# Moving PSUM copies to an idle engine, splitting the first loads and using a second PSUM bank in a four-layer attention kernel

## The chip, the cores and the metric

The kernel runs on one NeuronCore of one Trainium2 chip. The metric is the device time of one execution in microseconds (us); lower is better. Before the change it was 2143.56 us, the median of 12 runs (2141.75 to 2147.53). The profile has a row for each engine; they run side by side and meet at semaphores: PE (matmuls), with its weight loads in a row of their own (PEld), DVE (VectorE), ACT (ScalarE), POOL (GpSimd); SP issues the transfers. The program gives each engine one list. In the traces below VectorE and ScalarE work theirs off in order, so an instruction that waits also holds up what stands behind it.

## The reference

```python
S, D, H = 2048, 512, 32                       # head size 16
x = x + A(layernorm(x))                        # softmax attention, one K and V for all 32 heads
x = x + B(layernorm(x))                        # linear attention
x = x + A(layernorm(x)); x = x + B(layernorm(x))
# A: o = softmax(q k^T / 4) v, then @ wo
# B: phi(t) = where(t > 0, t + 1, exp(t)) + 1e-6
#    kv = phi(k)^T v ; z = sum phi(k) ; o = phi(q) kv / (phi(q) z + 1e-6), then @ wo
```

A block A needs 32 x 2048 x 2048 exponentials; in both kernels ScalarE does all of them. A block B has no such loop.

## The kernel before

The program first builds a plan: every operation is added with an engine, a planned time `tau` and the events that it waits for; then each engine's list is sorted by `tau` and emitted. The planned times only set the order; the semaphores decide the real times. The time line of one execution is: first prologue (layernorm, transposes, projections of all 16 tiles of 128 rows), attention loop, tail (preparation of B for the last tile), B main merged with the second prologue, second loop, second tail, final B main.

The loads: x is one transfer, and every projection waits for `ev_w`, the last of all weights.

```python
    ev_x = add(SP, 0.0, lambda e: e.dma_start(x_sb[:], xv), s_xdma, 16)
    ev_x.tau = 8.0
    add(SP, 0.01, ... wk_sb ...); add(SP, 0.02, ... wv_sb ...); add(SP, 0.03, ... wq_sb ...)
    # ... cut: wo_sb, wqkv_sb ...
    ev_w = add(SP, 0.06, lambda e: e.dma_start(wo2_sb[:], ...), s_wdma, 16)
    ev_w.tau = 12.0
```

PSUM is the memory that the matmuls write; the kernel uses it as banks 0 to 7. A session is a group of matmuls into one PSUM bank, and the instructions that read the bank ("readers"). A chain object orders the sessions of one bank: the next one waits for the last reader. In the prologue all copies out of PSUM are VectorE's.

```python
    def proj_session(chain, tau, mml, ncols, w_mm, readers):
        tp = chain.start_tau(_tmax(tau, list(w_mm)))
        # ... cut: 4 matmuls that accumulate into bank(chain.bank) ...
        for (eng, dtau, fn, sem_, xw) in readers:
            tr = _tmax(tr + dtau, [evm] + list(xw))
            evr = add(eng, tr, ..., sem_, waits=[evm] + list(xw))
            evs.append(evr)
        chain.last = evs[-1]
```

The nonlinearity `phi` of B: VectorE reads the bank twice (min, max), ScalarE takes the exponential of the min, VectorE adds. All sessions of the preparation of B use bank 7, because during the loop banks 0 to 5 hold scores and bank 6 the accumulator.

```python
        evs = proj_session(chain, _tmax(tau, w_m), mml, 512, w_mm, [
            (DV, 0.0, ... m_buf = min(src, 0) ...), (DV, D_EVQ, ... r_buf = max(src, 0) + 1e-6 ...)])
        ev_e = add(AC, ..., e.activation(e_buf[:, s, :], m_buf[:, s, :], ACTF.Exp), ac_a, waits=w_e)
        ev_add = add(DV, ..., dst = e_buf + r_buf, dv_a, waits=[ev_e, ev_r])
```

B main: 64 matmuls sum kv over all tiles, VectorE masks the result, and then for each tile: numerator and denominator (PE), two reciprocals and two products (DVE), four transposes (PE), a copy (DVE), the output projection (PE), the addition to x (DVE).

```python
        for g in range(NG8):
            for t in range(T):       # 64 matmuls, they wait for all of pk, v and pq
                ev_kvz = add(PE, tk, ... matmul(kvz_ap(g), lhsT=pk_tok[...], rhs=vaugB[...]) ...)
        # ... cut: mask, then for each tile t: ...
            evc = add(DV, ..., e.tensor_copy(OT_sb[:, t % 2, :, :], tpv), dv_a, waits=wc)
            # ... cut: 4 projection matmuls into bank 5 ...
            evx = add(DV, ..., x_sb[:, t, :] += bank(5), dv_x, waits=[evy])
```

The softmax here doesn't subtract the row's maximum and nothing guards it: scores larger than these inputs give would overflow.

Of the kernel before, what the change touches and what calls it, by code (L numbers as in the profile page):

```python
# [1 line left out]

# [37 lines left out]
class _Sched:  # L40
# [37 lines left out]
    def plan(self, tau, fn):  # L78
        heapq.heappush(self.heap, (float(tau), self.hseq, fn))
        self.hseq += 1  # L80

    def run(self):
        while self.heap:
            tau, _, fn = heapq.heappop(self.heap)
            fn()
# [39 lines left out]
def bass_interleave_layers__grouped_kv_mqa__linear_attn_block__prompt_kernel(  # L125
# [12 lines left out]
    P = 128  # L138
# [8 lines left out]
    EPS = 1e-3  # L147
    HOP = 0.25
# [89 lines left out]
    ev_x = add(SP, 0.0, lambda e: e.dma_start(x_sb[:], xv), s_xdma, 16)  # L238
    ev_x.tau = 8.0
    add(SP, 0.01, lambda e: e.dma_start(wk_sb[:], A_wk.rearrange("(ft f) c -> f ft c", f=P)), s_wdma, 16)  # L240
    add(SP, 0.02, lambda e: e.dma_start(wv_sb[:], A_wv.rearrange("(ft f) c -> f ft c", f=P)), s_wdma, 16)
    add(SP, 0.03, lambda e: e.dma_start(wq_sb[:], A_wq.rearrange("(ft f) c -> f ft c", f=P)), s_wdma, 16)
    add(SP, 0.04, lambda e: e.dma_start(wo_sb[:], A_wo.rearrange("(g r) c -> r g c", r=P)), s_wdma, 16)
    add(SP, 0.05, lambda e: e.dma_start(wqkv_sb[:], B_wqkv.rearrange("(ft f) c -> f ft c", f=P)), s_wdma, 16)
    ev_w = add(SP, 0.06, lambda e: e.dma_start(wo2_sb[:], B_wo.rearrange("(g r) c -> r g c", r=P)), s_wdma, 16)
    ev_w.tau = 12.0
# [20 lines left out]
    t_ = 12.5  # L267
    ev_wkrep = None
    for ft in range(FT):
        ev_wkrep = add(PO, t_, lambda e, ft=ft: e.tensor_copy(  # L270
            wk_rep[:, ft, :].rearrange("p (r d) -> p r d", r=8),
            wk_sb[:, ft, :].unsqueeze(1).to_broadcast([P, 8, DH])), po_a, waits=[ev_w] if ft == 0 else [])
        t_ += 0.5
# [3 lines left out]
    def ln_tile(t, x_ev, tau, chain):  # L277
        tau = _tmax(tau, [x_ev])
        ev1 = add(DV, tau, lambda e, t=t: e.bn_stats(stats[:, t, 0:6], x_sb[:, t, :]), dv_a, waits=[x_ev])  # L279
        ev2 = add(DV, tau + 0.7, lambda e, t=t: e.bn_aggr(mv[:, t, :], stats[:, t, 0:6]), dv_a, waits=[ev1])  # L280
        ev3 = add(DV, tau + 0.95, lambda e, t=t: e.tensor_scalar(out=veps[:, t:t + 1], in0=mv[:, t, 1:2], scalar1=1e-5, scalar2=None,  # L281
                                                             op0=ALU.add), dv_a, waits=[ev2])
        ev4 = add(PO, _tmax(tau + 1.35, [ev3, ev_mhalf]), lambda e, t=t: e.tensor_tensor(out=rstd[:, t:t + 1], in0=veps[:, t:t + 1], in1=mhalf[:, 0:1], op=ALU.pow),  # L283
                  po_a, waits=[ev3, ev_mhalf])
        slot = t % 2
        wr = ln_state["xn_last_reader"][slot]
        tx = _tmax(tau + 2.2, [ev4, wr])
        ev5 = add(DV, tx, lambda e, t=t, slot=slot: e.tensor_scalar(  # L288
            out=xn_buf[:, slot, :], in0=x_sb[:, t, :], scalar1=mv[:, t, 0:1], scalar2=rstd[:, t:t + 1],
            op0=ALU.subtract, op1=ALU.mult), dv_a, waits=[ev4, wr])  # L290
        tp = chain.start_tau(_tmax(tx + 0.4 + HOP, [ev5, ev_ident]))
        tpv = bank_bf(chain.bank)
        evt = None
        w0 = [ev5, chain.last, ev_ident]
        for ft in range(FT):
            evt = add(PE, tp + ft * EPS, (lambda e, ft=ft, slot=slot, tpv=tpv: e.transpose(tpv[:, ft, :], xn_buf[:, slot, ft * P:(ft + 1) * P], ident[:])),  # L296
                      pe_a if ft == FT - 1 else None, waits=(w0 if ft == 0 else []))
        ln_state["xn_last_reader"][slot] = evt
        evc = add(DV, evt.tau + 0.7 + HOP, lambda e, t=t, tpv=tpv: e.tensor_copy(xnT[:, :, t * P:(t + 1) * P], tpv), dv_a, waits=[evt])  # L299
        chain.last = evc  # L300
        return evc

    def proj_session(chain, tau, mml, ncols, w_mm, readers):
        tp = chain.start_tau(_tmax(tau, list(w_mm)))
        dst = bank(chain.bank, ncols)
        n = len(mml)
        evm = None
        w0 = [chain.last] + list(w_mm)
        for k, (l, r) in enumerate(mml):
            evm = add(PE, tp + k * EPS, (lambda e, l=l, r=r, k=k, n=n, dst=dst: e.matmul(dst, lhsT=l, rhs=r, start=(k == 0), stop=(k == n - 1))),  # L310
                      pe_a if k == n - 1 else None, waits=(w0 if k == 0 else []))
        evs = []
        tr = tp + n * min(D_MM, 0.05 + ncols * 0.0004) + HOP
        for (eng, dtau, fn, sem_, xw) in readers:
            tr = _tmax(tr + dtau, [evm] + list(xw))
            evr = add(eng, tr, (lambda e, fn=fn, dst=dst: fn(e, dst)), sem_, waits=[evm] + list(xw))
            evs.append(evr)
        chain.last = evs[-1]
        return evs

    def a_prologue(x_evs, tau0, R):
# [4 lines left out]
        chains = [chain6, chain7]  # L326

        def tile_task(t, tau_t):
            ch = chains[t % 2]
            ev_xnT = ln_tile(t, x_evs[t], tau_t, ch)  # L330
            R["xnT"][t] = ev_xnT
            mml = [(xnT[:, ft, t * P:(t + 1) * P], wv_sb[:, ft, :]) for ft in range(FT)]
            evs = proj_session(ch, ev_xnT.tau + HOP, mml, DH, [ev_xnT, ev_w],
                               [(DV, 0.0, (lambda e, src, t=t: e.tensor_copy(Vaug[:, t, 0:DH], src)), dv_a, [ev_ones])])
            R["V"][t] = evs[0]
            if t % 4 == 3:
                b = t // 4
                plan(ev_xnT.tau + HOP, lambda b=b: block_task(b))

        def block_task(b):  # L340
            xw = [R["xnT"][tt] for tt in range(4 * b, 4 * b + 4)] + [ev_w, ev_wkrep]
            tq = _tmax(0, xw, d=HOP)
            for g in range(NG8):
                chq = chains[(g + b) % 2]
                mml = [(wq_sb[:, ft, g * P:(g + 1) * P], xnT[:, ft, b * 512:(b + 1) * 512]) for ft in range(FT)]
                evs = proj_session(chq, tq, mml, 512, xw,
                                   [(DV, 0.0, (lambda e, src, g=g, b=b: e.tensor_copy(QT_sb[:, g, b * 512:(b + 1) * 512], src)), dv_a, [])])  # L347
                R["QT"][(g, b)] = evs[0]
                tq += 0.6
# [3 lines left out]
                               [(DV, 0.0, (lambda e, src, b=b: e.tensor_copy(Krep_sb[:, b * 512:(b + 1) * 512], src)), dv_a, [])])  # L353
            R["Krep"][b] = evs[0]

        for t in range(T):
            tau_t = max(tau0 + 1.7 * t, x_evs[t].tau + HOP)
# [9 lines left out]
    def a_loop(R, L0, on_x, pre_wait):  # L367
# [18 lines left out]
        def tau_seg(j):  # L386
            return L0 + (j + 1) * TG + 0.05

# [138 lines left out]
    def phi_session(chain, tau, mml, dst_ap, w_mm, act_slack):  # L527
# [5 lines left out]
        evs = proj_session(chain, _tmax(tau, w_m), mml, 512, w_mm, [  # L533
            (DV, 0.0, (lambda e, src, s=s: e.tensor_scalar(out=m_buf[:, s, :], in0=src, scalar1=0.0, scalar2=None, op0=ALU.min)), dv_a, w_m),  # L534
            (DV, D_EVQ, (lambda e, src, s=s: e.tensor_scalar(out=r_buf[:, s, :], in0=src, scalar1=0.0, scalar2=1e-6, op0=ALU.max, op1=ALU.add)), dv_a, []),  # L535
        ])
        ev_m, ev_r = evs
        w_e = [ev_m] + ([prev] if prev is not None else [])
        ev_e = add(AC, _tmax(ev_m.tau + act_slack, w_e), (lambda e, s=s: e.activation(e_buf[:, s, :], m_buf[:, s, :], ACTF.Exp)), ac_a, waits=w_e)  # L539
        ev_add = add(DV, _tmax(ev_e.tau + 0.7 + HOP, [ev_e, ev_r]), (lambda e, s=s, dst_ap=dst_ap: e.tensor_tensor(  # L540
            out=dst_ap, in0=e_buf[:, s, :], in1=r_buf[:, s, :], op=ALU.add)), dv_a, waits=[ev_e, ev_r])
        bstate["phi_last"][s] = ev_add
        return ev_add

    def b_prep_tile(t, x_ev, RB, act_slack, gap):
# [4 lines left out]

        def task_k():
            ev_xnT = RB["xnT"][t]
# [4 lines left out]
        def task_v():  # L557
# [3 lines left out]
                (DV, 0.0, (lambda e, src, t=t: e.tensor_copy(vaugB_v[:, t, :, 0:DH], src.rearrange("p (h d) -> p h d", d=DH))), dv_a, [ev_onesB])])  # L561
# [22 lines left out]
    def b_main(RB, tau0, prev_epi, x_out, on_x):  # L584
# [26 lines left out]
        for t in range(T):  # L611
# [4 lines left out]
            tb0 = _tmax(B0 + t * DB, w)  # L616
# [13 lines left out]
            td = _tmax(evnd.tau + 4 * 0.11 + HOP, wd)  # L630
# [12 lines left out]
            if t >= 1:  # L643
                wt.append(cp_ev[t - 1])
            tt = _tmax(evmul.tau + HOP, wt)
            tpv = bank_bf(4)
# [12 lines left out]
            evc = add(DV, _tmax(evt.tau + 0.7 + HOP, wc), (lambda e, t=t, tpv=tpv: e.tensor_copy(OT_sb[:, t % 2, :, :], tpv)), dv_a, waits=wc)  # L659
# [4 lines left out]
            ty = _tmax(evc.tau + HOP, wy)  # L664
# [6 lines left out]
            evx = add(DV, evy.tau + 4 * D_MM + HOP, (lambda e, t=t: e.tensor_tensor(out=x_sb[:, t, :], in0=x_sb[:, t, :], in1=bank(5), op=ALU.add)),  # L671
# [7 lines left out]
    x_evs = [ev_x] * T  # L679
    tau = 9.0  # L680
    prev_epi = {}
    i = 0
    while i < len(layers):
        L = layers[i]
        if L == "A":
# [6 lines left out]
            if nextB:  # L692
                def on_x(qt, evx, RB=RB):
                    b_prep_tile(qt, evx, RB, act_slack=8.0, gap=1.0)
# [7 lines left out]
            if nextB:  # L702
                tau0 = max(max(e.tau for e in x_evs) + 1.0, bprep_end(RB) + 0.5)
                x_out = [None] * T
                b_main(RB, tau0, prev_epi, x_out, None)
# [63 lines left out]
```

## Time and profile before

The stage table gives, for each stretch between two marks of the timeline, its length, and the busy time and the number of instructions of PE, PEld, DVE, ACT and POOL; then the clock that was granted to PE (1.00 is full), the busy share of the DMA engines and GB/s. The marks are: the first exponential of 128x1536, the last normalisation of the loop, the first masking of kv. Where two instructions of an engine overlap, the time counts once. An engine that goes from instruction to instruction can show a little under 100%, for the short gaps before an instruction that needs the result of the last one. The stage table of the kernel before:

```profile
0.00:68.20 68.20, 37.33 (x212) 16.73 (x213) 39.42 (x118) 1.30 (x2) 15.83 (x32) 0.90 0.24 78
68.20:1011.70 943.50, 788.74 (x10585) 468.92 (x10583) 200.22 (x583) 936.19 (x710) 8.24 (x15) 1.00 0.01 2
1011.70:1047.20 35.50, 20.75 (x100) 9.89 (x100) 13.51 (x25) 3.15 (x5) 0.55 (x1) 0.52 0.00 0
1047.20:1124.30 77.10, 56.00 (x405) 26.89 (x405) 69.55 (x218) 0.00 (x0) 8.80 (x16) 0.96 0.00 1
1124.30:2067.90 943.60, 788.77 (x10585) 468.86 (x10583) 200.25 (x584) 936.20 (x710) 8.24 (x15) 1.00 0.01 2
2067.90:2102.30 34.40, 19.68 (x100) 9.34 (x100) 13.48 (x26) 3.15 (x5) 0.55 (x1) 0.55 0.00 0
2102.30:2142.50 40.20, 26.90 (x192) 12.24 (x192) 34.86 (x100) 0.00 (x0) 0.00 (x0) 0.99 0.16 53
```

What to see: in the two loops (943.5 us each) ACT is busy for 936 us. They are bound by the exponentials. The other five stretches sum to 255.4 us, and ACT does nothing in them except the few exponentials of `phi` in the tails: 0.00 us in both B mains. DVE is the busy engine instead: 69.55 of 77.1 us, 34.86 of 40.2 us. The same on the page's rows, where each digit is the busy share of a fortieth of the span in tenths:

```profile
DVE  5221222112322232111680222322213121321227
ACT  0799999999999999998009999999999999999960
```

The first prologue: when PE's first projection starts, and what it waited for. The columns of a timeline line are the start, the duration, engine, line, operation, output<-input, shapes and, in brackets, the idle time of the engine before it and what ended it. Two lines of the timeline of the kernel before:

```profile
9.71 0.69 DVE L279 BATCH_NORM_STATS2 stats<-x_sb 128x6 f32<-128x512 bf16 x1 [9.71 <-DMA x_sb<-in_A_x_dram]
...
18.38 0.25 PE L310 MATMUL ps_all<-wv_sb,xnT 128*128 128x16 bf16 x4 [5.82 <-DMA wo_sb<-in_B_wo_dram]
```

x was there at 9.71, but the V projection of tile 0 waited until 18.38 for a weight that only the output projections of B need.

One session of the first tail, timeline of the kernel before:

```profile
1028.58 1.89 PE L310 MATMUL ps_all<-xnT,wqkv_sb 128*128 128x512 bf16 x4 [1.38 <-DVE r_buf L535]
...
1030.50 0.69 DVE L534 TENSOR_SCALAR m_buf<-ps_all 128x512 f32<-128x512 f32 x1 [1.98 <-PE ps_all L310]
1031.11 0.68 DVE L535 TENSOR_SCALAR r_buf<-ps_all 128x512 f32<-128x512 f32 x1
1031.23 0.63 ACT L539 ACTIVATE e_buf<-m_buf 128x512 f32<-128x512 f32 x1 [2.64 <-DVE m_buf L534]
...
1031.85 1.89 PE L310 MATMUL ps_all<-xnT,wqkv_sb 128*128 128x512 bf16 x4 [1.38 <-DVE r_buf L535]
```

Matmul 1.89 us, min 0.69, max 0.68, next matmul: 3.27 us from one to the next, all in a row, at a granted clock of 0.50. The exponential runs beside it and is hidden.

The merged stage, one long stretch of the stage table of the kernel before: DVE 49.40 of 50 us.

```profile
1060.00:1110.00 50.00, 38.15 (x293) 18.84 (x294) 49.40 (x162) 0.00 (x0) 7.15 (x13) 1.00 0.00 1
```

The final B main, timeline of the kernel before: from one copy to the next 2.18 us, and DVE goes from instruction to instruction.

```profile
2133.80 0.42 DVE L659 COPY OT_sb<-ps_all 128x512 bf16<-128x512 bf16 x1
...
2135.98 0.42 DVE L659 COPY OT_sb<-ps_all 128x512 bf16<-128x512 bf16 x1
```

### The profile page before, as it was taken

How to read it: one execution, taken by the hardware profiler on the slowest of the kernel's cores; microseconds unless marked ns; L12 is line 12 of the kernel's file. 1: busy time of each engine (PE TensorE's matmuls, PEld its weight loads, DVE VectorE, ACT ScalarE, POOL GpSimd, SP SyncE). 2: the span in 40 equal slices, each digit the busy share in tenths (PEclk: the TensorE clock that was granted, in tenths of full speed). 3: DMA queues.
4: the chain of work that ended last, by engine and by line, in shares of the span. 5: the costliest groups of instructions: out<-in, count | busy, mean ns of one | idle time of the engine just before them, and what ended most of it. 6: DMA issues, size and time to landing. Idle time of an engine off the chain costs nothing.

```text
span 2142.5 us, 49091 instructions
## 1 busy us (share of the span) xinstructions
PE 1738.2 (81%) x22176; PEld 1012.9 (47%) x22176; DVE 571.3 (27%) x1648; ACT 1880.0 (88%) x1431; POOL 42.2 (2%) x80
## 2 busy tenths in 40 slices
PE   4888888888888888887678888888888888888876
PEld 2454554445454554544334544544544454444533
DVE  5221222112322232111680222322213121321227
ACT  0799999999999999998009999999999999999960
POOL 2000000000000000000010000000000000000000
PEclk9999999999999999999799999999999999999988
DMA  3000000000000000000000000000000000000001
GB/s 99 1 2 2 2 2 2 2 2 1 2 2 2 2 2 2 2 1 2 1 1 2 2 1 2 2 2 1 2 2 1 2 2 2 1 2 2 1 1 40
DMA packets 7745, 10.50 MB, mean 5 GB/s; under 512 B 1392, under 2 KB 7024, under 8 KB 7536
## 3 DMA queue, kind: packets, MB, share of 16 engines
q1 hardware_dynamic: 7536, 7.37, 1.1%
q8 instruction: 173, 2.83, 0.6%
q14 instruction: 36, 0.29, 0.0%
HBM read 5.28 MB, written 2.10 MB: 3 GB/s over the span
## 4 chain that ended last, share of the span: by engine, by line
ACT 42%; PE 37%; issue 11%; DVE 9%; DMA 0%; SPq 0%; POOL 0%; ACTq 0%; POOLq 0%
ACT PT L433 41%; PE ps_all L423 21%; PE ps_all L452 8%; PE ps_all L310 5%; PE ps_all L508 1%; ACT e_buf L539 1%; DVE Osb L637 1%; DVE Osb L475 1%; DVE x_sb L671 1%; DVE rdenA L469 1%; DVE stats L279 1%; DVE QT_sb L347 1%; PE ps_all L593 1%; DVE rdenB L635 1%; PE ps_all L296 0%
## 5 line engine op out<-in xcount | busy, mean ns | idle before, releaser
L433 ACT ACTIVATE PT<-ps_all 128x1536 bf16<-128x1536 f32 (+1 forms) x1366 | 1851.5, 1490 | 165.8 <-PE ps_all L423 163.9
L423 PE MATMUL ps_all<-qbd,Krep_sb 128*128 128x512 bf16 x4096 | 1114.8, 381 | 215.4 <-ACT PT L433 215.2
L452 PEld LDWEIGHTS ps_all<-Vaug,PT 128*128 128x128 bf16 x16384 | 619.6, 96 | 432.8 <-DVE Osb L475 110.8
L452 PE MATMUL ps_all<-Vaug,PT 128*128 128x17 bf16 x16384 | 639.9, 171 | 93.0 <-DVE Osb L475 91.1
L423 PEld LDWEIGHTS ps_all<-qbd,Krep_sb 128*128 128x128 bf16 x4096 | 301.2, 97 | 488.7 <-ACT PT L433 269.0
L469 DVE RECIPROCAL rdenA<-ps_all 128x4 f32<-128x4 f32 x256 | 46.7, 183 | 1152.1 <-PE ps_all L452 1152.1
L406 DVE TENSOR_TENSOR qbd<-QT_sb,mask 128x512 bf16<-128x512 bf16 x256 | 102.3, 415 | 0.0
L539 ACT ACTIVATE e_buf<-m_buf 128x512 f32<-128x512 f32 x64 | 41.3, 646 | 47.1 <-DVE m_buf L534 47.1
L283 POOL TENSOR_TENSOR rstd<-veps,mhalf 128x1 f32<-128x1 f32 x64 | 35.2, 550 | 2024.4 <-DVE veps L281 2014.8
L310 PE MATMUL ps_all<-wqkv_sb,xnT 128*128 128x512 bf16 x256 | 68.9, 393 | 3.8 <-DVE r_buf L535 2.8
L534 DVE TENSOR_SCALAR m_buf<-ps_all 128x512 f32<-128x512 f32 x64 | 44.2, 690 | 82.3 <-PE ps_all L310 82.3
L475 DVE TENSOR_TENSOR Osb<-ps_all,rdenA 128x64 bf16<-128x64 f32 x256 | 57.4, 224 | 8.9
L540 DVE TENSOR_TENSOR pk_tok<-e_buf,r_buf 128x512 bf16<-128x512 f32 x32 | 22.1, 691 | 104.2 <-ACT e_buf L539 104.2
L310 PE MATMUL ps_all<-xnT,wqkv_sb 128*128 128x512 bf16 x128 | 39.8, 441 | 11.0 <-DVE r_buf L535 9.1
L279 DVE BATCH_NORM_STATS2 stats<-x_sb 128x6 f32<-128x512 bf16 x64 | 44.1, 689 | 10.9 <-DMA x_sb<-in_A_x_dram 9.7
L310 PE MATMUL ps_all<-xnT,wq_sb 128*128 128x512 bf16 x128 | 41.1, 465 | 6.9 <-DVE QT_sb L347 3.4
L296 PE MATMUL ps_all<-ident,xn_buf 128*128 128x128 bf16 x256 | 27.6, 236 | 22.4 <-DVE xn_buf L288 19.4
L535 DVE TENSOR_SCALAR r_buf<-ps_all 128x512 f32<-128x512 f32 x64 | 43.5, 680 | 0.0
L667 PE MATMUL ps_all<-wo_sb,OT_sb 128*128 128x512 bf16 x128 | 33.1, 381 | 9.2 <-DVE OT_sb L659 9.2
L508 PE MATMUL ps_all<-wo_sb,OT_sb 128*128 128x512 bf16 x128 | 33.9, 388 | 1.0 <-DVE OT_sb L496 1.0
L511 DVE TENSOR_TENSOR x_sb<-x_sb,ps_all 128x512 bf16<-128x512 bf16 x32 | 22.0, 687 | 46.7 <-PE ps_all L508 46.7
L299 DVE COPY xnT<-ps_all 128x512 bf16<-128x512 bf16 x64 | 26.1, 408 | 24.7 <-PE ps_all L296 24.7
(46 smaller groups left out, 417.9 us busy)
## 6 DMA issues: line engine op xcount, KB each, us to landing
x_sb<-in_A_x_dram SPq DMA_DIRECT2D x1, 2048.0 KB, 8.9
out_dram<-x_sb SPq DMA_DIRECT2D x16, 128.0 KB, 1.7
wqkv_sb<-in_B_wqkv_dram SPq DMA_DIRECT2D x1, 1536.0 KB, 8.9
wq_sb<-in_A_wq_dram SPq DMA_DIRECT2D x1, 512.0 KB, 6.5
wo_sb<-in_A_wo_dram SPq DMA_DIRECT2D x1, 512.0 KB, 6.5
wo_sb<-in_B_wo_dram SPq DMA_DIRECT2D x1, 512.0 KB, 9.2
wk_sb<-in_A_wk_dram SPq DMA_DIRECT2D x1, 16.0 KB, 8.3
wv_sb<-in_A_wv_dram SPq DMA_DIRECT2D x1, 16.0 KB, 6.7
```

The source lines that it names most:

```text
L279: ev1 = add(DV, tau, lambda e, t=t: e.bn_stats(stats[:, t, 0:6], x_sb[:, t, :]), dv_a, waits=[x_ev])
L310: evm = add(PE, tp + k * EPS, (lambda e, l=l, r=r, k=k, n=n, dst=dst: e.matmul(dst, lhsT=l, rhs=r, start=(k == 0), stop=(k == n - 1))), pe ...
L406: qbd_ready[u] = add(DV, tq, (lambda e, u=u, qt=qt, g=g, half=half: e.tensor_tensor(out=qbd[:, u % NQBD, :].rearrange("p (a b) -> p a b", ...
L423: ev = add(PE, tsi, (lambda e, dst=dst, t=t, u=u: e.matmul(dst, lhsT=Krep_sb[:, t * P:(t + 1) * P], rhs=qbd[:, u % NQBD, :], start=True, s ...
L433: e_done[j] = add(AC, _tmax(tau_E(j), w), (lambda e, j=j, ng=ng, b0=b0: e.activation(PT[:, j % NPT, 0:ng * 512], bank(b0, ng * 512), ACTF. ...
L452: ev = add(PE, tpv, (lambda e, col0=col0, j=j, idx=idx, hh=hh, t=t: e.matmul(ps_all[:, col0:col0 + 17], lhsT=PT[:, j % NPT, idx * 512 + hh ...
L469: evr = add(DV, tn, (lambda e, accv=accv: e.reciprocal(rdenA[:, :].unsqueeze(2), accv[:, :, DH:DH + 1])), dv_a, waits=[ev_acc])
L475: acc_free[u] = add(DV, _tmax(tn + EPS / 4, wn, d=EPS / 8), (lambda e, qt=qt, quad=quad, accv=accv: e.tensor_tensor(out=Osb[:, qt % 2, qua ...
L508: evy = add(PE, t2 + g * EPS, (lambda e, g=g, qt=qt: e.matmul(bank(7), lhsT=OT_sb[:, qt % 2, g, :], rhs=wo_sb[:, g, :], start=(g == 0), st ...
L534: (DV, 0.0, (lambda e, src, s=s: e.tensor_scalar(out=m_buf[:, s, :], in0=src, scalar1=0.0, scalar2=None, op0=ALU.min)), dv_a, w_m),
L535: (DV, D_EVQ, (lambda e, src, s=s: e.tensor_scalar(out=r_buf[:, s, :], in0=src, scalar1=0.0, scalar2=1e-6, op0=ALU.max, op1=ALU.add)), dv_ ...
L539: ev_e = add(AC, _tmax(ev_m.tau + act_slack, w_e), (lambda e, s=s: e.activation(e_buf[:, s, :], m_buf[:, s, :], ACTF.Exp)), ac_a, waits=w_e)
```

## The change

The intent is to use the idle ScalarE and PSUM banks outside the loops, and to start earlier:

1. x comes in four transfers; V, Q and K of A wait only for wk, wv and wq, which are issued before the rest of x; the plan starts earlier.
2. Copies out of PSUM (xnT, V, Q, K, the transposed output of B) go to ScalarE where the plan says that it is free, which is everywhere except from 2 us ahead of a loop to its end.
3. In the tails, `phi` uses relu (the max with 0) on ScalarE, and two banks alternate.
4. The final B main lets the transposes lag two tiles, with two banks for them, and shifts some planned times.

Two smaller edits to the plan are not in the cut below: the tiles of a prologue are planned 1.35 us apart instead of 1.7, and for the last tiles of a loop the planned distances of the preparation of B are shortened (`gap` 1.0 to 0.2, `act_slack` 8.0 to 0.3).

The heap code, rewritten by hand, runs when the program is built; it costs no device time.

```diff
+    act_busy = []
+    def act_free(tau):
+        for (a, b) in act_busy:
+            if a - 2.0 <= tau <= b:
+                return False
+        return True
+    def copy_op(tau, out_ap_fn, waits, prefer_act=True):
+        if prefer_act and act_free(tau):
+            return add(AC, tau, lambda e: out_ap_fn(e, True), ac_a, waits=waits)
+        return add(DV, tau, lambda e: out_ap_fn(e, False), dv_a, waits=waits)
-    ev_x = add(SP, 0.0, lambda e: e.dma_start(x_sb[:], xv), s_xdma, 16)
+    x_chunk(0, 0.0)
     # wk, wv
+    ev_wa = add(SP, 0.03, ... wq_sb ..., s_wdma, 16)
+    for c in range(1, 4):
+        x_chunk(c, 0.03 + 0.001 * c)
     # wo, wqkv, wo2 on another semaphore: ev_w
-        evc = add(DV, evt.tau + 0.7 + HOP, ... tensor_copy(xnT ...) ..., dv_a, waits=[evt])
+        evc = copy_op(evt.tau + 0.7 + HOP, cp, [evt])
     # ... cut: the same for V, Q, K; ev_wa in place of ev_w ...
+        L_end = tau_E(NGR) + 0.5
+        act_busy.append((L0, L_end))
+        if act_free(tau):                                       # phi, in the tails
+            evs = proj_session(chain, tau, mml, 512, w_mm, [
+                (AC, 0.0, ... r_buf = Relu(src) ..., ac_a, w_m),
+                (DV, 0.6, ... m_buf = min(src, 0) ..., dv_a, w_m),
+            ], serial=True)                                     # min waits for relu
+            # exp of m_buf on ScalarE, then DVE: dst = (e_buf + 1e-6) + r_buf
+        def task_tail():                                        # last tile
+            chT = Chain(0)
+            chT.last = astate["e_done"][-1]
+            chs = [chain7, chT]
+            # k on chs[0], v on chs[1], the four q on chs[g % 2]
     # B main
-            tpv = bank_bf(4)
+            tpv = bank_bf(4 if not final or t % 2 == 0 else 6)
-            evc = add(DV, ..., tensor_copy(OT_sb ...), dv_a, waits=wc)
+            evc = copy_op(..., OT_sb ..., wc)
     # ... cut: with final, the wait cp_ev[t - 2] for cp_ev[t - 1], and planned times shifted ...
```

## The prediction

> **What bounds it now.** The timeline splits the 2142.5 us into: first prologue 0 to 68.2 (the first 128x1536 exponential starts there), attention loop 68.2 to 1011.3, tail of linear-attention preparation 1011 to 1048, B main merged with the second prologue 1048 to 1124, loop 1124 to 2067, second tail to 2103, final B main to 2142. In both loops ScalarE is 10.0 of 10 us busy (stretch table), 1.345 us per exponential group. The change leaves the loops alone: inside them its guard sends copies back to VectorE. All gain must come from the other 256 us.
>
> **Step by step.**
>
> 1. First prologue. PE waits 5.8 us for the last weight DMA (wait list): tile 0's V matmul could start at 18.4 although its x was there at 9.7. After: x in four chunks, and V/Q/K wait only for wk, wv, wq. wq landed 11.5 behind 2 MB of x; behind 0.5 MB I estimate 9 to 9.5. Gain about 9. From there the 16 tiles took 50 us, 3.1 each, with VectorE about 75% busy. The 52 PSUM copies (0.41, 0.17, 0.69 us) go to an idle ScalarE. Its exponential of 128x512 takes 0.65 us; the Trainium skill, "ScalarE: Activation LUTs", What ACT_TABLE_LOAD costs, gives 186 ns + 0.833 ns per element, 0.61 us, for any function; so I take 0.6. The two PSUM banks then bind: per four tiles and bank, two tiles at 1.9 us and 2.5 projections at 1.75 (warm PE) to 2.55 (cold): 2.05 to 2.55 per tile; with in-order stalls 2.5. Loop starts near 50: gain 18.
>
> 2. Each tail. Six projection sessions share bank 7: 1.89 us of cold matmul, then two 0.69 us VectorE reads, 3.27 us per session (timeline); 21.5 us from first projection to the kv matmuls. After: two banks alternate, so the matmul hides, but relu (0.63), min (0.69) and exp (0.65) form a serial loop over ScalarE and VectorE of about 2.0 us per session. I estimate 14.5: gain 7 each, plus about 0.5 if a denser PE runs the kv matmuls (6.3 us) at a higher clock. The skill, "TensorE: Matmul & The Clock Gate", Part 1, says sustained activity releases the half clock; the trace agrees: 1.89 us for four 512-column matmuls at granted clock 0.5 in the tail, 1.04 at 1.0 after it.
>
> 3. B main with second prologue. VectorE is 95 to 100% busy from 1050 to 1110, 3.9 us per tile. The change moves about 1.4 us per tile (at the pitch of back-to-back instructions, 0.33, 0.33, 0.09, 0.6) to ScalarE: VectorE's floor falls to 42 us of 62, but PE's own work is about as long, so stalls appear. I expect 50. The last block's 14 us to the loop stays. Gain 12.
>
> 4. Final B main. VectorE bound, 2.17 us per tile; less the 0.33 us copy, 1.84, if the two-tile lag hides latency. Gain 4.
>
> Sum 18+14+1+12+4 = 49: **2095 us**, 8-in-10 range 2076 to 2116. Chances: faster by over 2% 0.70, within 2% 0.29, slower 0.01.
>
> **Right if:** first big exponential near 50; first to last of the tail 7 shorter; loops still 943 each; in B main VectorE at 80 to 90%, no longer 100%; matmuls then wait for ScalarE copies.
>
> **Wrong if:** wq lands later than 10; PE stays cold throughout the prologue (loop start 55); in-order ScalarE or PE queues in the merged stage stall one another (gain under 8) or overlap perfectly (up to 19); relu/copy cause extra table loads (1.28 us each); the tail's new loop is cheaper, PE warming, or dearer because min waits for relu; the final lag brings stalls.

## The result, and the profile after

The changed kernel took 2095.84 us, the median of 8 runs (2095.18 to 2096.96). The ratio of times is 0.9778 (95% interval 0.9768 to 0.9787). The stage table of the changed kernel, with the same marks:

```profile
0.00:49.30 49.30, 33.05 (x213) 15.52 (x214) 20.45 (x67) 23.70 (x54) 15.46 (x32) 0.93 0.34 108
49.30:992.80 943.50, 788.72 (x10585) 468.83 (x10583) 199.48 (x580) 936.16 (x710) 8.24 (x15) 1.00 0.01 2
992.80:1020.10 27.30, 16.54 (x100) 9.29 (x100) 9.63 (x19) 6.86 (x12) 0.55 (x1) 0.69 0.00 1
1020.10:1086.10 66.00, 51.88 (x404) 27.61 (x405) 49.43 (x151) 31.38 (x68) 8.79 (x16) 0.95 0.00 1
1086.10:2029.70 943.60, 788.71 (x10585) 468.82 (x10583) 199.54 (x581) 936.20 (x710) 8.24 (x15) 1.00 0.01 2
2029.70:2057.10 27.40, 17.12 (x100) 9.88 (x100) 9.56 (x18) 6.86 (x12) 0.55 (x1) 0.69 0.00 1
2057.10:2093.70 36.60, 25.13 (x192) 13.49 (x192) 30.36 (x84) 9.38 (x16) 0.00 (x0) 1.00 0.17 58
```

Each line answers to the same line of before:

| stretch | before, us | after, us | difference | predicted |
|---|---|---|---|---|
| first prologue | 68.2 | 49.3 | -18.9 | -18 |
| two loops | 943.5, 943.6 | 943.5, 943.6 | 0 | 0 |
| two tails, with the kv matmuls | 35.5, 34.4 | 27.3, 27.4 | -15.2 | -15 |
| B main merged with second prologue | 77.1 | 66.0 | -11.1 | -12 |
| final B main | 40.2 | 36.6 | -3.6 | -4 |

The page's rows of the changed kernel:

```profile
DVE  3022232111321232111641122322113122322116
ACT  5999999999999999999369999999999999999982
```

The first digit of ACT went from 0 to 5, and the two slices in the middle (the 20th and 21st) from 0 0 to 3 6: ScalarE now works there, and the second loop, too, begins within the later of the two. In the first prologue (timeline of the changed kernel):

```profile
5.00 1.29 DVE L328 BATCH_NORM_STATS2 stats<-x_sb 128x6 f32<-128x512 bf16 x2 [5.00 <-DMA x_sb<-in_A_x_dram]
...
9.09 0.28 PE L363 MATMUL ps_all<-wv_sb,xnT 128*128 128x16 bf16 x4 [0.20 <-ACT xnT L350]
```

Layernorm starts at 5.00 instead of 9.71 and V at 9.09 instead of 18.38. What V waits for now is no longer a transfer but the ScalarE copy of its own input.

A little more than one session of the first tail (timeline of the changed kernel):

```profile
1007.17 0.58 ACT L609 ACTIVATE r_buf<-ps_all 128x512 f32<-128x512 f32 x1
...
1007.90 0.68 DVE L610 TENSOR_SCALAR m_buf<-ps_all 128x512 f32<-128x512 f32 x1
1008.62 0.63 ACT L614 ACTIVATE e_buf<-m_buf 128x512 f32<-128x512 f32 x1 [0.87 <-DVE m_buf L610]
...
1008.64 1.04 PE L363 MATMUL ps_all<-xnT,wqkv_sb 128*128 128x512 bf16 x4 [0.95 <-DVE m_buf L610]
1009.16 0.58 ACT L609 ACTIVATE r_buf<-ps_all 128x512 f32<-128x512 f32 x1
1009.28 0.69 DVE L615 SCALAR_TENSOR_TENSOR pqT<-e_buf,r_buf 128x512 bf16<-128x512 f32 x1 [0.70 <-ACT e_buf L614]
1009.89 0.68 DVE L610 TENSOR_SCALAR m_buf<-ps_all 128x512 f32<-128x512 f32 x1
1010.61 0.63 ACT L614 ACTIVATE e_buf<-m_buf 128x512 f32<-128x512 f32 x1 [0.87 <-DVE m_buf L610]
```

The matmul (1.04 us, at the full clock by now) runs beside the readers. Relu 1007.17, min 1007.90, exp 1008.62, next relu 1009.16: 1.99 us, as forecast. But look at which wait ends last for the next min, at 1009.89. It stands without a gap behind the add of 1009.28, which waited for exp. The relu of its bank had ended at 1009.74; hand-overs between these two engines cost 0.03 to 0.04 us here (min to exp, exp to add), so the relu was out of the way about 0.1 us early. The loop that binds is min, exp, add, and the next min behind the add in VectorE's order: 0.72 + 0.66 + 0.61 = 1.99 us. The relu only nearly binds.

The merged stage, two stretches of the stage table of the changed kernel; the first without a projection block, the second with one:

```profile
1028.40:1040.20 11.80, 7.88 (x83) 4.63 (x81) 11.52 (x37) 5.36 (x12) 2.20 (x4) 1.00 0.01 1
1040.20:1060.00 19.80, 18.69 (x148) 10.20 (x146) 17.63 (x55) 11.51 (x25) 3.30 (x6) 1.00 0.00 1
```

In the first, DVE is busy for 11.52 of 11.8 us and PE for 7.88. In the second PE is busy for 18.69 of 19.8 us and DVE for 17.63. The limit alternates.

The final B main, timeline of the changed kernel:

```profile
2072.50 0.59 ACT L766 COPY OT_sb<-ps_all 128x512 bf16<-128x512 bf16 x1 [1.31 <-PE ps_all L756]
...
2074.39 0.59 ACT L766 COPY OT_sb<-ps_all 128x512 bf16<-128x512 bf16 x1 [1.30 <-PE ps_all L756]
```

From copy to copy 1.89 us, where it was 2.18.

### The profile page after: what moved, and what is told of

It is laid out like the page before. It is cut to its first block, busy times and chain, and to the rows that moved or that the text cites. A ratio compares the mean times of both kernels' runs of the same rounds, so it can differ in the third digit from the quotient of the medians.

```text
span 2093.7 us, 49127 instructions
## 1 busy us (share of the span) xinstructions
PE 1721.1 (82%) x22176; PEld 1013.4 (48%) x22176; DVE 518.4 (25%) x1498; ACT 1950.5 (93%) x1581; POOL 41.8 (2%) x80
## 4 chain that ended last, share of the span: by engine, by line
ACT 44%; PE 39%; issue 11%; DVE 5%; DMA 0%; POOL 0%; ACTq 0%; POOLq 0%; DVEq 0%
ACT PT L506 42%; PE ps_all L496 22%; PE ps_all L525 8%; PE ps_all L363 5%; PE ps_all L581 1%; ACT e_buf L624 1%; DVE Osb L548 1%; DVE Osb L743 1%; DVE rdenA L542 1%; DVE x_sb L778 1%; PE ps_all L345 1%; PE ps_all L699 1%; PE ps_all L774 1%; ACT xnT L350 0%; DVE rdenB L741 0%
## 5 line engine op out<-in xcount | busy, mean ns | idle before, releaser
L542 DVE RECIPROCAL rdenA<-ps_all 128x4 f32<-128x4 f32 x256 | 46.7, 183 | 1174.6 <-PE ps_all L525 1174.6
L363 PE MATMUL ps_all<-wqkv_sb,xnT 128*128 128x512 bf16 x256 | 68.6, 393 | 1.4 <-ACT xnT L350 1.4
L766 ACT COPY OT_sb<-ps_all 128x512 bf16<-128x512 bf16 x32 | 18.9, 589 | 48.6 <-PE ps_all L756 48.5
L619 DVE TENSOR_SCALAR m_buf<-ps_all 128x512 f32<-128x512 f32 x54 | 37.3, 690 | 63.7 <-PE ps_all L363 63.7
L350 ACT COPY xnT<-ps_all 128x512 bf16<-128x512 bf16 x34 | 19.8, 588 | 27.3 <-PE ps_all L345 27.0
L363 PE MATMUL ps_all<-xnT,wqkv_sb 128*128 128x512 bf16 x128 | 34.3, 395 | 3.9 <-DVE m_buf L610 2.8
L620 DVE TENSOR_SCALAR r_buf<-ps_all 128x512 f32<-128x512 f32 x54 | 36.7, 680 | 0.0
L624 ACT ACTIVATE e_buf<-m_buf 128x512 f32<-128x512 f32 x54 | 35.0, 648 | 0.0
```

Of the source, the lines that this page charges most:

```text
L363: evm = add(PE, tp + k * eps, (lambda e, l=l, r=r, k=k, n=n, dst=dst: e.matmul(dst, lhsT=l, rhs=r, start=(k == 0), stop=(k == n - 1))), pe ...
L542: evr = add(DV, tn, (lambda e, accv=accv: e.reciprocal(rdenA[:, :].unsqueeze(2), accv[:, :, DH:DH + 1])), dv_a, waits=[ev_acc])
L624: ev_e = add(AC, _tmax(ev_m.tau + act_slack, w_e), (lambda e, s=s: e.activation(e_buf[:, s, :], m_buf[:, s, :], ACTF.Exp)), ac_a, waits=w_e)
```

## The experiments

Twelve kernels ran, all correct. Ten are the changed kernel with one edit, the eleventh joins three edits, and the last is the changed kernel again. They were run on several chips, each beside the kernel before on the same chip, so the ratios compare best; stage times are from one profiled execution each. Stages that an edit does not touch varied from profile to profile: the first prologue from 48.7 to 50.9 us, the merged stage from 63.7 to 66.7, the final stage from 36.6 to 38.0. For the merged stage this goes in part with the clock granted in its last 13 us, where PE computes the last projections ahead of the loop: 0.74 in the trace of the changed kernel (66.0 us), 0.87 in its second (65.4; other runs at 0.87 up to 66.7), 1.00 in the run with one bank in the tail (63.7). A difference of a stage below 2 us is therefore not taken as shown by one profile.

### First prologue: loads undone

```diff
-    x_chunk(0, 0.0)
+    ev_x = add(SP, 0.0, lambda e: e.dma_start(x_sb[:], xv), s_xdma, 16)
+    ev_x.tau = 8.0
+    x_dma_evs.extend([ev_x] * T)
-    for c in range(1, 4):
-        x_chunk(c, 0.03 + 0.001 * c)
-    ev_w.tau = 16.0
+    ev_w.tau = 12.0
+    ev_wa = ev_w
     # ... cut: all weights on one semaphore, a planned time, the test for the first prologue ...
-    tau = 3.0
+    tau = 9.0
```

> The changed kernel with the old loads: x as one transfer, every projection waiting for the last weight, the old start times in the plan; the copies stay on ScalarE. Theory (start and copies are two separate gains in the first prologue): V can start only at 18.4 instead of 9.1, and the 40.2 us from there to the loop stay, so the first big exponential comes at about 58 instead of 49.3, and the whole takes about 9 us more than the changed kernel (about 2105). Rival (the copies alone did it, the start is hidden): first big exponential within 2 us of 49.3.

Measured: 2104.61 us, ratio 0.9817 (0.9803 to 0.9832). PE's V projection waits for the last weight again, and the first big exponential comes at 60.14 (timeline of this run):

```profile
18.30 0.25 PE L364 MATMUL ps_all<-wv_sb,xnT 128*128 128x16 bf16 x4 [5.82 <-DMA wo_sb<-in_B_wo_dram]
...
60.14 2.79 ACT L507 ACTIVATE PT<-ps_all 128x1536 bf16<-128x1536 f32 x2
```

The loads are worth 10.9 us of the prologue (60.14 - 49.27) and 8.8 us of the whole (2104.61 - 2095.84). The copies did not do it alone.

### First prologue: copies on VectorE

```diff
-    act_busy = []
+    act_busy = [(0.0, 1e9)]
-        act_busy.append((L0, L_end))
+        act_busy[:] = [(L0, L_end)]
```

> The changed kernel with the first prologue's 52 PSUM copies on VectorE again; the new loads stay. Theory (two separate gains): the old pace of 3.1 us per tile from 9.1 on, first big exponential at about 59, whole about 2105. Rival (the two PSUM banks alone set the pace; a VectorE copy is no longer than a ScalarE copy, and VectorE was only 75% busy): first big exponential within 3 us of 49.3.

Measured: 2103.89 us, ratio 0.9812 (0.9797 to 0.9826). The stage table of the run, from V to the first big exponential at 58.45:

```profile
9.00:58.40 49.40, 35.39 (x206) 15.76 (x205) 35.01 (x106) 0.00 (x0) 8.24 (x18) 0.86 0.19 67
```

The first V projection came at 9.49, as early as in the changed kernel, but the pace is the old one: (58.45 - 9.49) / 16 = 3.06 us per tile. So the copies are worth 9.2 us of the prologue (8.1 of the whole), although a copy of xnT takes 0.59 us on ScalarE against 0.41 on VectorE, and although VectorE was busy for a little over two thirds of the stretch. The rival, which looked at the banks and the durations alone, falls. What fits is that a copy on VectorE must also wait its turn among the layernorms of later tiles, while the bank and PE wait for it. The traces show this wait: from the end of the matmuls that a copy reads to its start, the 52 copies waited 19.3 us in sum in this run, 13.7 in the kernel before, 4.7 in the changed kernel (the copies of xnT 0.66 us each in this run, 0.08 in the changed kernel). By duration alone the move would not pay: the 16 copies of xnT are longer on ScalarE by 2.9 us in sum, the 20 of 512 columns in fp32 shorter by 2.0. That this queue, and nothing else, is the cause was not tested by itself. The two parts, 10.9 and 9.2, add up to 20.1, near the 18.9 that the change gained.

### Tail: one bank

```diff
-            chs = [chain7, chT]
+            chs = [chain7, chain7]
```

> The changed kernel with all six sessions of each tail in the one PSUM bank again; relu stays on ScalarE. Theory (the second bank hides the matmul, that is the gain): per session 1.89 cold matmul, relu 0.6, min 0.69 and hops, about 3.3 us; from first projection to the kv matmuls 20 to 21.5 us instead of 13.8, whole about 14 us more (2110). Rival (moving relu off VectorE was the gain): 16 us or less, whole at most 5 us more.

Measured: 2109.37 us, ratio 0.9841 (0.9824 to 0.9857). From the first projection to the kv matmuls 20.94 us in both tails, where the changed kernel has 13.84 and 14.23. With one bank, relu on ScalarE gains 0.6 us per tail over the kernel before (21.51). The second bank is the gain; this run keeps the shortened planned distances, so these are not.

### Tail: two banks, both reads on VectorE

```diff
-        if act_free(tau):
+        if False:
             evs = proj_session(chain, tau, mml, 512, w_mm, [   # relu on ScalarE
```

> The changed kernel with two banks in the tail, but min and max both on VectorE as before, and the addition as before. Theory (the second bank is the gain, and relu on ScalarE only trades one serial loop for another): VectorE has three instructions of about 0.61 pitch per session, 1.83, against the 1.98 measured for relu-min-exp; from first projection to the kv matmuls 12 to 14.5 us, whole within 3 us of the changed kernel. Rival (relu on ScalarE is worth its 0.6 us per session): 3 to 4 us more per tail, whole 6 to 8 us more.

Measured: 2096.3 us, ratio 0.9777 (0.9762 to 0.9791), the same as the changed kernel. First projection to kv matmuls 12.98 and 13.56 us, 0.9 and 0.7 less than the changed kernel's. One session (timeline of this run):

```profile
1006.68 0.68 DVE L619 TENSOR_SCALAR m_buf<-ps_all 128x512 f32<-128x512 f32 x1
1007.29 0.68 DVE L620 TENSOR_SCALAR r_buf<-ps_all 128x512 f32<-128x512 f32 x1
1007.40 0.63 ACT L624 ACTIVATE e_buf<-m_buf 128x512 f32<-128x512 f32 x1 [1.37 <-DVE m_buf L619]
...
1008.07 0.69 DVE L625 TENSOR_TENSOR pqT<-e_buf,r_buf 128x512 bf16<-128x512 f32 x1
1008.68 0.68 DVE L619 TENSOR_SCALAR m_buf<-ps_all 128x512 f32<-128x512 f32 x1
```

From min to min 2.00 us, with no relu anywhere. It is the same loop as in the changed kernel: min, exp, add, next min. VectorE's third instruction, the max, fits into the time in which it waits for exp. Given the second bank, moving relu to ScalarE brings nothing. The Trainium skill, "ScalarE: Activation LUTs", Rules for kernel authors, would leave relu on VectorE, and names its speed in bf16. Here the operand is fp32 in PSUM, the two are about equally long (0.58 us relu on ScalarE, 0.68 max on VectorE), and what decides is the order in which the two engines wait for each other.

### Tail: exp straight from PSUM

min(exp(t), 1) + max(t, 0) is the same function without a min ahead of the exponential. ScalarE reads the bank twice, one after the other, and VectorE does one pass. The 1e-6 is dropped in the tails.

```diff
-                (DV, 0.6, ... m_buf = min(src, 0) ..., dv_a, w_m),
-            ], serial=True)
+                (AC, 0.5, ... e_buf = Exp(src) ..., ac_a, w_m),
+            ])
-            # dst = (e_buf + 1e-6) + r_buf
+            # dst = min(e_buf, 1.0) + r_buf
```

> The changed kernel, with another form of the nonlinearity in the tails only: ScalarE reads PSUM twice (relu, then exp of the unclamped value), and VectorE does min(exp, 1) plus relu in one pass; the added 1e-6 is dropped there. No instruction of ScalarE then waits for VectorE. Theory (the 1.98 us per session of the changed tail is the loop relu, min on VectorE, exp, next relu): about 1.1 us per session, first projection to kv matmuls 10 to 11.5 us instead of 13.8 and 14.2, whole 5 to 8 us less than the changed kernel. Rival (the matmuls of a half-clocked PE bind the tail at 1.75 us per session): 13 us or more, whole within 2 us.

Measured: 2086.68 us, ratio 0.9736 (0.9721 to 0.975). From the relu of one session to the next now 1.1 us (timeline of this run):

```profile
1007.68 0.60 ACT L609 ACTIVATE r_buf<-ps_all 128x512 f32<-128x512 f32 x1
1008.18 0.59 ACT L610 ACTIVATE e_buf<-ps_all 128x512 f32<-128x512 f32 x1
1008.81 0.60 ACT L609 ACTIVATE r_buf<-ps_all 128x512 f32<-128x512 f32 x1
```

First projection to kv matmuls 10.59 and 10.65 us. Without the min ahead of exp there is no way back from VectorE to ScalarE, and ScalarE's two reads set the pace. So the loop between the two engines, and not the matmul or the bank, set the 1.99 us. The whole gained more than expected, 9 us, because the kv matmuls behind it took 3.99 us instead of 5.97 and 6.52: PE's clock was at 1.00 in them.

A version of the changed kernel in which relu and min read the bank at the same time (two engines on bank 7 with nothing that orders them) did not run. The Trainium skill, "PSUM — Partial Sum Buffer", PSUM bank collisions, says that the hardware does not arbitrate such reads; no run here shows it.

The loop might also be broken by planning the min of the next session ahead of the add of this one. That was not tried, so what it would give stays open.

### Tail: kv sums early

The 60 kv matmuls of tiles 0 to 14 need nothing of the last tile. They go into banks 1 to 4, free since the last exponentials of the loop, one matmul group per bank.

```diff
+            if t == T - 1:
+                kv_early(x_ev.tau + 0.9, 30)       # while the last tile is normalised
             ev_xnT = ln_tile(t, x_ev, x_ev.tau + 1.0, chain7)
+                kv_early(ev_xnT.tau - 0.5, 8)      # while xnT is copied
+                kv_early(t0 + 1.4 * (g + 2) + 0.6, 8)   # after each q session
 # b_main: only the four matmuls of tile 15 are left; they and the mask wait for pk and v, not pq
-            return bank(g // 2, 136, (g % 2) * 136)
+            return bank(1 + g, 136)
```

> The changed kernel, and the 60 kv matmuls of tiles 0 to 14 issued while the last tile is still being prepared, into four PSUM banks that the finished attention loop has left (two matmul groups no longer share a bank); only the four of the last tile stay behind. Theory (in the tail PE is idle most of the time and runs at half clock for that; the 6 us of kv matmuls and the 1 us of masking stand at its end only because they are issued there): from the last normalisation of the loop to the first B main matmul each tail gets 6 to 9 us shorter, the whole 12 to 18 us shorter than the changed kernel (2078 to 2084), and the first projections of the tail run at the full clock. Rival (the early matmuls stand in the way of the last tile's own chain, or the clock stays at half): less than 8 us in all.

Measured: 2080.57 us, ratio 0.969 (0.9674 to 0.9706), 15.3 us under the changed kernel by the medians, as the theory had it. From the last normalisation to the first B main matmul 19.5 us in the first tail, 28.2 in the changed kernel. Two lines of the timeline of this run:

```profile
996.84 3.51 PE L643 MATMUL ps_all<-vaugB,pk_tok 128*128 128x136 bf16 x30
...
1001.25 1.90 PE L363 MATMUL ps_all<-wqkv_sb,xnT 128*128 128x512 bf16 x8 [0.20 <-ACT xnT L350]
```

The eight matmuls of the first two projections take 1.90 us; in the changed kernel they take 3.60. The work that fills PE's gap also goes with a higher clock; how much of the gain is the earlier start and how much the clock was not separated. The Trainium skill, "TensorE: Matmul & The Clock Gate", Part 1, tells of a half clock that sustained activity lifts; this pair of numbers agrees with it.

### Merged stage: output copies on VectorE, and second prologue's copies on VectorE

```diff
-            evc = copy_op(..., OT_sb ..., wc)
+            evc = copy_op(..., OT_sb ..., wc, prefer_act=final)
```

> The changed kernel with one of the two groups of moved copies of the merged stage (first B main with the second prologue) taken back: the 16 copies of the transposed output go to VectorE again, the prologue's copies stay on ScalarE. Theory (VectorE's own work binds the stage where no projection block runs; a period there is 2.96 us and VectorE is 98% busy in it): a period of about 3.3, the merged stage 3 to 5.5 us longer than the 66.0 of the changed kernel. Rival (PE binds the stage after the change, VectorE has slack): less than 1.5 us longer.

```diff
+        pro_act[0] = tau0 < 5.0        # a_prologue: copies on ScalarE in the first one only
     # ... cut: back to True at each loop; True for the output copies ...
-        if prefer_act and act_free(tau):
+        if (pro_act[0] if prefer_act is None else prefer_act) and act_free(tau):
```

> The changed kernel with the other group taken back: the second prologue's 52 copies go to VectorE, the output copies stay on ScalarE. Theory (VectorE work): about 1.2 us more VectorE work per tile, the merged stage 8 to 12 us longer than 66.0, VectorE about 95% busy in its first 60 us again. With the run before, the two parts should add up to about the 11 us that the change gained here. Rival (PE binds): less than 4 us longer.

Measured: with the output copies back, 2098.16 us, ratio 0.9786 (0.9771 to 0.98), the stage 68.6 us, 2.5 longer at the same clock in its last 13 us (0.74); the period where no block runs is 3.16 us instead of 2.96. With the prologue's copies back, 2102.46 us, ratio 0.9811 (0.9797 to 0.9826), the stage 72.7 us, DVE busy for 56.3 of its first 60 us. That is 6.7 longer than in the changed kernel's trace, or 9.0 longer than in the one unedited stage that also ended at the full clock. In the whole times the two edits cost 2.3 and 6.6 us, 8.9 together, less than expected; the 2.3 is not clear of the noise, since the two intervals of the ratio overlap. VectorE's work is a limit of this stage (both rivals named smaller numbers), but not the only one: the 16 output copies, at 0.33 us from one instruction to the next, are 5.3 us of VectorE work, and moving them gave 2.5 in these traces.

### Merged stage: projections spread

```diff
-                tq += 0.6
+                tq += 0.6 if tau0 < 5.0 else 1.8
```

> The changed kernel with the five projections of a block planned 1.8 apart instead of 0.6 in the second prologue only, so that they spread over the next four tiles. Theory (what kept the merged stage at 66.0, where VectorE's work alone would allow about 55, is that PE is 94% busy while a block runs, VectorE 98% where none does; the limits alternate instead of overlapping): the merged stage 3 to 6 us shorter. Rival (the in-order queues, not the bunching, cost the rest): less than 1 us, or longer.

Measured: 2094.6 us, ratio 0.9759 (0.9744 to 0.9774), the stage 64.1 us. Beside the changed kernel's 66.0 that looks like a gain of 1.9, but the clock differs. The last 13 us of the stage, first in the changed kernel, then in this run (stage tables):

```profile
1073.10:1086.10 13.00, 9.86 (x49) 4.09 (x48) 2.62 (x8) 5.70 (x12) 0.55 (x1) 0.74 0.00 0
```

```profile
1071.60:1084.60 13.00, 10.43 (x62) 4.48 (x62) 3.37 (x9) 7.11 (x16) 0.78 (x2) 1.00 0.00 0
```

PE's clock was 0.74 there and 1.00 here. The run with one bank in the tail, whose merged stage is unedited, also had 1.00, and needed 63.7 us. At equal clock, then, no gain is seen, and the two intervals of the ratio overlap. The run is inconclusive: it neither shows nor rules out a gain of a microsecond, and whether spreading raises the clock at the end can't be told: the combined kernel below, which spreads them too, also had 1.00 there, but so had two kernels that don't (one bank in the tail; the second prologue's copies on VectorE).

### Final B main: old order, copy on ScalarE

```diff
-                b_main(RB, tau0, prev_epi, x_out, None, final=(i + 2 >= len(layers)))
+                b_main(RB, tau0, prev_epi, x_out, None, final=False)
```

> The changed kernel with the final B main in the old order: no lag of two tiles, one bank for the transposes, no delays in the plan; its output copy stays on ScalarE. Theory (the copy alone gives nothing because the chain transpose, copy, projection, addition has no slack; the lag is what makes the 0.33 us of VectorE work come out): a period of about 2.2 us instead of 1.90, the final stage about 4 us longer than 36.6. Rival (VectorE's work alone sets the period): final stage within 1 us of 36.6.

Measured: 2096.86 us (2095.89 to 2101.85), ratio 0.979 (0.9774 to 0.9806); the final stage 39.9 us. The period is 2.07 us (two transposes of neighbouring tiles in the timeline of this run):

```profile
2068.98 0.40 PE L756 MATMUL ps_all<-ident,Osb 128*128 128x128 bf16 x4
...
2071.05 0.40 PE L756 MATMUL ps_all<-ident,Osb 128*128 128x128 bf16 x4
```

So of the 0.28 us per tile (2.18 to 1.90) the moved copy alone brings 0.11 and the lag 0.17. That the copy alone would give nothing was too strong. In the whole time the lag's 16 x 0.17 = 2.7 us did not come out: the median is 1.0 us above the changed kernel's, the intervals overlap, and the final stage itself was 36.6 us in one trace of the changed kernel and 38.0 in another. The difference of the period is clear; that of the whole is not.

### Three findings together, and the changed kernel again

Exp from PSUM, kv sums early and spread projections in one kernel, five rounds, beside the unedited changed kernel on the same chip.

> The changed kernel with three findings together: in the tails exp straight from PSUM and the early kv matmuls, in the second prologue the spread projections. Theory (each takes away another wait: the loop between ScalarE and VectorE, the late start of the kv matmuls with the half clock, the bunching): from the last normalisation of the loop to the first B main matmul about 15.5 us instead of 28.2, the whole 2066 to 2075 us, 20 to 30 us under the changed kernel run beside it. Rival (they draw on the same wait, so they do not add up): 2077 or more.

> The changed kernel itself, unedited, on the same chip as the combined one, for a direct comparison: 2094 to 2098 us, and the same stage times as in its first trace within 1.5 us each.

Measured: the combined kernel 2074.34 us (2073.96 to 2075.57), ratio 0.9679 (0.9666 to 0.9692); the changed kernel 2095.76 us (2094.25 to 2097.02), ratio 0.9777 (0.9764 to 0.979). 21.4 us less than the changed kernel and 69.3 less than the kernel before: it beats both. From the last normalisation to the first B main matmul 17.0 us in its first tail, 1.5 more than hoped. The three alone had given about 9, 15 and 1 us by the medians, 25 in sum; by the ratios 9, 19 and 4, because the kernel before took 2146.32 us on the chip of the last two. They do not add up in full, as the rival said, though the time stays under its 2077. The first two probably overlap: with exp from PSUM the kv matmuls already ran faster, and early kv sums take most of them out of the way, which can only be won once. Which share of the 21.4 the spread projections have is open.

## Why the prediction was right

The time was forecast to 1 us, and each term of the sum to 1.1 us. That the stages agree so closely is partly luck, since stages that no edit touched differed by 1.4 to 3 us from trace to trace. The terms stand on tested causes, but in two of them the reason was named less well than the size, as told below.

1. **First prologue: right (18 forecast, 18.9 measured).** Both halves, the start and the pace, were tested and are about equal. One size inside was off: wq was to land at 9 to 9.5, but it was issued at 2.38 and landed 5.1 us later, at 7.5. V starts at 9.09 anyway, because layernorm and copy of tile 0 are not done earlier: here the right start came from the wrong wait, by luck. The pace was 40.2 / 16 = 2.5 us per tile, as forecast. The reason given for it, two banks with their readers, was incomplete: the run with the copies on VectorE has the same banks and keeps 3.06, so the banks alone don't set the pace. What the traces show in its place is the copies' wait behind VectorE's other work, 19.3 us in sum with the copies on VectorE and 4.7 on ScalarE, though no run tested it by itself.
2. **Tails: right in size (15 forecast, 15.2 measured), the loop misnamed.** The step that failed is "relu (0.63), min (0.69) and exp (0.65) form a serial loop over ScalarE and VectorE of about 2.0 us per session". The 2.0 was there (1.99), but the loop is min, exp, add. With both reads on VectorE it stayed at 2.00 without any relu; with the min gone it fell to 1.1. That relu, min and exp also sum to nearly 2.0 made the wrong loop give the right number. The gain itself is the second bank's: with one bank the tail kept 20.9 of its 21.5 us. The kv matmuls were to gain 0.5 us in each tail; they took 6.0 and 6.5 us after, 6.4 and 6.1 before. That gain is not there: the two tails' sum came out right because the projections gained 7.7 and 7.3 us for the 7 forecast.
3. **Merged stage: right in size (12 forecast, 11.1 measured).** DVE fell to 46.7 of 53 us, 88%, in the range named. One of its signs came only in part: matmuls were to wait for ScalarE copies, and PE does so for 5.1 us in all (1.8 of them for xnT), but its longest waits in this stage are still for VectorE (9.1 us in all, 6.4 of them for the products ahead of the transposes).
4. **Final stage: right (4 forecast, 3.6 measured),** with a period of 1.90 us for 1.84. In the second trace of the changed kernel, at a lower clock for some 6 us of this stage, the gain was 2.2.
5. **Loops: unchanged, as forecast,** to 0.1 us.

No extra table load appeared: both profiles have one, of 1.28 us, before the first exponential or copy.

## What to carry to other kernels

Ask of each stage which engine idles there, not of the whole: ScalarE was 88% busy, and yet it did nothing for nearly 250 us of the five stages outside the loops. An operation may be worth moving to an engine that is slower at it, if what it waits for is its turn in a busy in-order queue. Where two engines hand results back and forth within one step, count the loop, not the work, and close it through the instruction that really stands ahead in the engine's order: a second bank or a moved instruction only helps until that loop is the limit, and the form of the arithmetic (exp before min) can take it away.

## What the Trainium skill lacked or had wrong

- "ScalarE: Activation LUTs", Rules for kernel authors, sends relu to VectorE and gives its speed in bf16 as the reason; the row says nothing of fp32 operands in PSUM. For 128x512 in fp32 read from PSUM, ScalarE's relu took 0.58 to 0.60 us and its copy 0.57 to 0.59, VectorE's min 0.69, max 0.68 and copy 0.69; the copy from bf16 was shorter on VectorE (0.41 against 0.59).
- "ScalarE: Activation LUTs", What ACT_TABLE_LOAD costs: worked out from the formula, 512 elements are estimated at 0.61 us, with an overlap of 0.09; measured 0.57 to 0.60 for reads from PSUM, and 1.07 us for two copies in a row, so an overlap of 0.11. The exponential took 0.63 to 0.65 us from the SBUF buffer `m_buf` and 0.59 from PSUM, so where the operand lies matters, which this formula leaves out. Close enough to cost with.
- "TensorE: Matmul & The Clock Gate", Part 1, gives the windows but not the busy share that keeps the clock up. In the tail of the kernel before, a matmul burst of 1.89 us in every 3.27 stayed at 0.50 for 20 us; in the loops, PE 84% busy, it stayed at 1.00. The clock also fell early in the final stage: 0.69 to 0.74 for about 6 us in the second trace of the changed kernel, 1.00 in the first, which goes with 38.0 against 36.6 us for that stage.
- No page was found that gives the time that issuing a transfer takes behind another one: with 2 MB of x in front, SP needed 2.11, 1.48 and 1.45 us for wk, wv and wq; with 0.5 MB in front, 0.50, 0.50 and 0.51.
